# A 160-column last slot, chosen on chip, in an attention, mixture-of-experts and maxout kernel

## The chip, the cores and the metric

The kernel runs on one core of one Trainium2 chip. The metric is the device time of one execution in microseconds (us). The five engines run their own instruction streams in order: TensorE (PE, with its weight loads as PEld), VectorE (DVE), ScalarE (ACT), GpSimd (POOL) and SyncE (SP, which here issues DMAs).

## The reference

Three stages follow one another on 3072 tokens (4 sequences of 768) of width 384, all in float32:

```python
state = w * state + k_t v_t          # recurrent linear attention, 8 heads of 48
y_t = r_t @ (state + u * k_t v_t)
logits = x @ w_gate + modality_bias[modality_id]
e_idx = argmax(logits)               # one of 8 experts for each token
out[mask] = gate_w[mask] * (relu(x[mask] @ w1[e]) @ w2[e])      # 384 -> 1024 -> 384
h = maximum(maximum(x @ w1, x @ w2), x @ w3)                    # 384 -> 768
return h @ w_out                                               # 768 -> 384
```

The last stage's weights are 64-bit floats and arrive as their bit patterns; the gate's weights are scaled by 4.021, which makes the routing uneven. Worked out from the reference's own inputs (seed 0), the experts get 1569 (expert 6), 1354 (expert 5) and 149 tokens (expert 4), and the other five get none.

## The kernel before

The attention stage runs in 24 tiles of 128 tokens. After two thirds of them the most frequent expert so far is found, so that its weights are loaded while the rest of the attention runs. The expert stage then works in *slots*: a slot is one group of tokens of one expert. The first three slots (numbers 0 to 2 here) have 256 columns and belong to that expert when it has at least 768 tokens. The width of the slots behind them is chosen on chip among 256, 272, ... 384 (`WIDTHS`, nine of them) from the counts. `counting` (L607 to L645) makes that choice on DVE during slot 0: it counts how many slots each width would need, weighs them, and writes `sel`, a number that is read by all five engines (`chosen`, L1284) at the end of slot 0. The program holds one straight copy of the remaining slots for each width and each of two kinds (L1318): an *exact* copy, which has just the least number of slots that this width can need (`sure_slots`), and one which goes on in a chain of conditions. `sel` = 2 x width + kind is the number of the copy. With the counts above, 272 columns and nine slots behind the first three are chosen, the exact copy: slots 3 to 5 for the rest of expert 6, 6 to 10 for expert 5, slot 11 for expert 4.

A slot (`slot`, L1001) has eight steps. Step f makes 9 matmuls of the first layer for 128 of the 1024 hidden units (`first`, L943: three parts of 128 of the input, each as high x high, low x high and high x low of a split into two halves), which ACT (L946) and DVE (L947) turn into the high and the low half of `hid`; then 9 matmuls of the second layer for step f-1 (`second`, L955). So `hid` of step f is used one step later. Ahead of the last step the next slot's tokens are transposed on PE, three blocks of 128 at 272 columns (`turn`, L892), and split by ACT (L894) and DVE (L895). Where the slot behind belongs to another expert, each step's `renew` converts a part of that expert's weights: ACT makes the high half (L864), POOL or DVE the low half (L868).

Other work rides in the slots, handed out by position in the code: `slot` takes a list `side` and spreads it over its steps (`cum`). The list has the *conversion* of the last stage's weights (`converters`, L1029 to L1071): 24 pieces of 128 x 384, each of six jobs with seven DVE instructions (L1057 to L1068) on the landing buffers `m2raw`, and one POOL addition (L1062); and the *landing* jobs (`landing`), which work out where each result row belongs. Before, the 144 conversion jobs are spread over the nine slots 3 to 11, 16 in each; in the last slot the 24 `inv_out` matmuls (L555) stand too. The last stage (`run`) then works in six groups of 512 tokens until the end.

Each engine takes its instructions in the order of the code, so a DVE job that stands ahead of a `hid` instruction delays it.

Of the kernel before, what the change touches and what calls it, by code (L numbers as in the profile page):

```python
# [16 lines left out]
ALU = mybir.AluOpType  # L17
AX = mybir.AxisListType
# [5 lines left out]
P = 128  # L24
# [4 lines left out]
E = 8  # L29
SLOT = 256  # L30
WIDTHS = tuple(range(SLOT, SLOT + P + 1, P // 8))
NW = len(WIDTHS)
WIDE = WIDTHS[-1]
NJW = (NT - SLOT) // SLOT + 1
OWN = WIDE // P
AHEAD = 3


def last_slot(w):
    return AHEAD + (NT - SLOT - E) // w + E  # L40


def sure_slots(w):
    return AHEAD - (-(NT - AHEAD * SLOT) // w)
# [340 lines left out]
class Routing:  # L385
# [222 lines left out]
    def counting(self, wk):  # L608
        nc, V = self.nc, self.nc.vector
        tile = lambda shape, nm, dt=F32: wk.tile(shape, dt, tag=f"rt_{nm}", name=f"rt_{nm}")  # L610
        some = tile([P, 1, E], "all", BF16)
        self.tally(NTILE, some)
        cps = self.bank("cps")
        yield
        cnt = self.counts(wk, NTILE, some, cps)
        row = cnt.rearrange("p e o -> p o e")
        rem = tile([P, 1, E], "rem")
        V.tensor_tensor(rem, row, self.off, op=ALU.subtract)
        key = tile([P, 1, E], "key")
        V.scalar_tensor_tensor(key, row, float(E), self.prio, op0=ALU.mult, op1=ALU.add)  # L620
        over = tile([P, NW, E, NJW], "over", F16)
        for i in range(NW):
            V.tensor_tensor(over[:, i], rem[:, 0, :].unsqueeze(2).to_broadcast([P, E, NJW]),
                            self.wj[:, i:i + 1, :].to_broadcast([P, E, NJW]), op=ALU.is_gt)
            if i in (2, NW - 1):
                yield
        per = tile([P, NW, E], "per")
        V.tensor_reduce(per, over, axis=AX.X, op=ALU.add)
        num = tile([P, NW], "num")
        V.tensor_reduce(num, per, axis=AX.X, op=ALU.add)  # L630
        cost = tile([P, NW], "cost")
        V.tensor_tensor(cost, num, self.wcost, op=ALU.mult)
        yield
        V.tensor_tensor(cost, cost, self.wsel, op=ALU.add)
        least = tile([P, 1], "least")
        V.tensor_reduce(least, cost, axis=AX.X, op=ALU.min)
        pick = tile([P, NW], "pick")
        V.tensor_scalar(pick, cost, least, None, op0=ALU.is_equal)
        V.tensor_tensor(num, num, self.wsure, op=ALU.is_gt)
        V.scalar_tensor_tensor(num, self.wsel, 2.0, num, op0=ALU.mult, op1=ALU.add)  # L640
        V.tensor_tensor(num, num, pick, op=ALU.mult)
        V.tensor_reduce(least, num, axis=AX.X, op=ALU.add)
        V.tensor_copy(self.sel, least[0:1])
        self.plan = row, key, per, pick
        yield  # L645
# [169 lines left out]
class Experts:  # L815
# [5 lines left out]
    def open(self, st):  # L821
        tc = self.tc
        pool = st.enter_context(tc.tile_pool(name="mx", bufs=1))
        self.xg = [[pool.tile([P, DM], F32, name=f"xg{i}_{a}") for a in range(2)] for i in range(2)]
        self.xh, self.xl = ([pool.tile([P, KC, WIDE], F32R, name=f"{q}0")] for q in ("xh", "xl"))
        self.raw = (pool.tile([P, KC, FF], F32, name="raw1"), pool.tile([P, KF, DM], F32, name="raw2"))
        self.w = {nm: pool.tile(shape, F32R, name=f"w_{nm}")
                  for nm, shape in (("h1", [P, KC, FF]), ("l1", [P, KC, FF]), ("h2", [P, KF, DM]), ("l2", [P, KF, DM]))}
        self.hid = pool.tile([P, 4 * WIDE], F32R, name="hid")

# [47 lines left out]

    def gather(self, k, n=WIDE):
        for a in range(-(-n // P)):  # L880
# [32 lines left out]
    def open_more(self, pool):  # L913
        for i in range(2):
            self.xg[i] += [pool.tile([P, DM], F32, name=f"xg{i}_{a}") for a in range(2, OWN)]
        self.xh.append(pool.tile([P, KC, WIDE], F32R, name="xh1"))
        self.xl.append(pool.tile([P, KC, WIDE], F32R, name="xl1"))

# [79 lines left out]
        if job is not None:  # L998
            job(f)

    def slot(self, k, n, stop, total, side=()):  # L1001
        r = self.regs(k, stop)
        sure = sure_slots(n)

        def when(i, what):
            if i < min(sure, stop):
                what()
            elif i < stop:
                with self.tc.If(total > i):
                    what()  # L1010

        cum = [len(side) * c // 18 for c in (0, 3, 6, 9, 12, 15, 17, 18, 18)]
        for f in range(KF):
            if f == KF - 1:
                when(k + 1, lambda: self.turn(k + 1, n))
            self.step(k, f, n, r)
            if f == 0:
                when(k + 2, lambda: self.gather(k + 2, n))
            for j in side[cum[f]:cum[f + 1]]:
                j()  # L1020
        self.tail = (k, n, r)
# [178 lines left out]
def build(tc, aps):  # L1200
    nc = tc.nc
    ET = mybir.EngineType
    with ExitStack() as st:
# [4 lines left out]
        with tc.manual_schedule(), ExitStack() as right, ExitStack() as left:  # L1208
            att = Attention(tc, aps, const, ps, dram, x_dram)
            moe = Experts(tc, aps, att.ident, ps, x_dram)  # L1210
# [4 lines left out]
            route = moe.rt = Routing(tc, const, ps)  # L1215
            mo = MaxOut(tc, aps, route, ps)
            side = route.setup()
            every = (ET.PE, ET.Activation, ET.DVE, ET.Pool, ET.SP)
# [8 lines left out]
            for s in range(NTILE):  # L1227
                att.step(s, hook)
                if s == EARLY + 1:
                    for _ in side:  # L1230
                        pass
                    side = route.opening(rw, att.logits, att.bias, EARLY, lambda: moe.load_all(
                        moe.value(route.toptab[:, 0:1], (ET.SP,), E - 1)))
# [19 lines left out]
            def during(f):  # L1253
                if f < 3:
                    moe.split(f + 1, 0, nc.gpsimd)
                    moe.split(f + 1, 1)
                if f == 0:
                    with tc.If(odd > 0):
                        att.restore(EARLY, NTILE)
                    tally.append(route.choose(rw, att.logits, att.bias, EARLY, NTILE))  # L1260
                    next(tally[0])
                if f == 1:
                    next(tally.pop(), None)
                    top.close()
                    m2 = right.enter_context(tc.tile_pool(name="m2", bufs=1, side="right", reuse_waits="tile"))
                    moe.open_rows(m2)
                    moe.open_more(left.enter_context(tc.tile_pool(name="mx2", bufs=1, reuse_waits="tile")))
                    tally.append(brief.enter_context(tc.tile_pool(name="rq", bufs=1, reuse_waits="tile")))
                    tally.append(route.counting(tally[0]))
                if f > 1:  # L1270
                    next(tally[1], None)
                if f == 3:
                    moe.fetch_early(2)
                if f == 5:
                    with tc.If(moe.many > 0):
                        moe.turn(1)
# [4 lines left out]
            for _ in tally:  # L1281
                pass
            moe.tail = (0, SLOT, still)
            chosen = moe.value(route.sel, every, 2 * NW - 1)  # L1284
            ahead = lambda: tc.switch_hint({e: chosen for e in every}, 2 * NW, "width")
            with tc.If(moe.many > 0) as both:
                places = route.placing(rw)
                for k in range(1, AHEAD):
# [18 lines left out]
            total = moe.tab(0, NSLOT, every, NSLOT)  # L1307
# [7 lines left out]
            conv = mo.converters(left.enter_context(tc.tile_pool(name="m2tmp", bufs=1, reuse_waits="tile")))  # L1315
            jobs, finals = route.landing(mo.land, att.logits)

            for i in tc.Switch({e: chosen for e in every}, 2 * NW, "width"):  # L1318
                n, exact = WIDTHS[i // 2], i % 2 == 0
                sure = sure_slots(n)  # L1320
                stop = sure if exact else last_slot(n)
                moe.tail = (AHEAD - 1, SLOT, moe.regs(AHEAD - 1, stop))
                for k in range(AHEAD, sure):
                    a, b = (len(conv) * q // (sure - AHEAD) for q in (k - AHEAD, k - AHEAD + 1))
                    c, d = (len(jobs) * q // (sure - AHEAD - 1) for q in (k - AHEAD, k - AHEAD + 1))
                    side = conv[a:b]
                    for q, j in enumerate(jobs[c:d]):
                        side.insert(7 * q + 3, j)
                    if k == sure - 1:
                        for q, j in enumerate(finals):  # L1330
                            side.insert(3 * q + 1, j)
                    moe.slot(k, n, stop, total, side)
                if exact:
                    moe.end()
                    continue

                def more(k):
                    if k == stop:
                        moe.end()
                        return  # L1340
                    tail = moe.tail
                    with tc.If(total > k) as going:
                        moe.slot(k, n, stop, total)
                        more(k + 1)
                    moe.tail = tail
                    with going.Else():
                        moe.end()

                more(sure)
# [55 lines left out]
```

## Time and profile before

| | |
|---|---|
| median of 3 runs (lowest to highest) | 710.0 us (706.09 to 712.63) |
| the profiled execution | 708.11 us |
| its span, first to last instruction | 706.4 us |
| mean granted TensorE clock | 0.986 |
| PE, DVE, POOL, ACT busy | 95%, 58%, 34%, 33% of the span |
| expert slots 0 to 11 | from 146.1 to 396.0 us of the span |
| last stage | from 401 us to the end |

The PE share is of overlapping, pipelined matmuls: what a matmul costs is read from the distance between starts (in the chain of waits, nine matmuls in a row of 1.13 us are 125 ns each), not from its own duration.

### The profile page before, as it was taken

How to read it: one execution, taken by the hardware profiler on the slowest of the kernel's cores; microseconds unless marked ns; L12 is line 12 of the kernel's file. 1: busy time of each engine (PE TensorE's matmuls, PEld its weight loads, DVE VectorE, ACT ScalarE, POOL GpSimd, SP SyncE). 2: the span in 40 equal slices, each digit the busy share in tenths (PEclk: the TensorE clock that was granted, in tenths of full speed). 3: DMA queues.
4: the chain of work that ended last, by engine and by line, in shares of the span. 5: the costliest groups of instructions: out<-in, count | busy, mean ns of one | idle time of the engine just before them, and what ended most of it. 6: DMA issues, size and time to landing. Idle time of an engine off the chain costs nothing.

```text
span 706.4 us, 13754 instructions
## 1 busy us (share of the span) xinstructions
PE 669.1 (95%) x5046; PEld 598.5 (85%) x5046; DVE 409.7 (58%) x849; ACT 230.2 (33%) x545; POOL 238.8 (34%) x257
## 2 busy tenths in 40 slices
PE   8898998998989999999999899999999999999995
PEld 4787876788988989999989788888888888888884
DVE  6999998867647788777696655222222222322321
ACT  3765763652222243222242343221121221211211
POOL 6877764372033258323165211120210210210202
PEclk9999998999999999999999999999999999999998
DMA  8988867510024551333721000000100100100101
GB/s 219 299 251 249 267 196 225 193 52 23 1 73 124 169 168 55 110 97 88 217 68 47 3 1 0 12 34 0 46 0 1 45 0 1 45 0 1 45 0 46
DMA packets 36253, 61.33 MB, mean 87 GB/s; under 512 B 4881, under 2 KB 24977, under 8 KB 36161
## 3 DMA queue, kind: packets, MB, share of 16 engines
q1 hardware_dynamic: 32512, 49.02, 23.2%
q0 software_dynamic: 3648, 11.21, 5.1%
q8 instruction: 43, 0.70, 0.4%
q14 instruction: 50, 0.40, 0.2%
HBM read 50.77 MB, written 9.44 MB: 85 GB/s over the span
## 4 chain that ended last, share of the span: by engine, by line
PE 44%; issue 11%; DVE 2%; POOL 1%; ACT 0%; POOLq 0%; DVEq 0%; ACTq 0%
PE l L1135 24%; PE o L1160 7%; PE acc L955 6%; PE h L943 6%; POOL out_dram L1171 1%; PE inv_out L555 1%; PE t L892 0%; DVE m2wo L1065 0%; DVE hid L947 0%; DVE m2wl L1099 0%; DVE x2l L1099 0%; POOL x2l L1122 0%; PE acc L892 0%; POOLq L1401 0%; DVE m2wo L1057 0%
## 5 line engine op out<-in xcount | busy, mean ns | idle before, releaser
L1139 DVE TENSOR_TENSOR tm<-tm,l 128x512 f32<-128x512 f32 x72 | 49.4, 687 | 174.5 <-PE l L1135 174.5
L955 PE MATMUL acc<-hid,w_h 128*128 128x272 f32 (+1 forms) x576 | 124.9, 290 | 7.4 <-DVE hid L947 5.8
L1135 PE MATMUL l<-x2h,m2wh 128*128 128x512 f32 x324 | 126.2, 390 | 1.8 <-ACT m2wh L1103 1.8
L1135 PE MATMUL l<-x2l,m2wh 128*128 128x512 f32 x324 | 127.5, 395 | 0.4 <-DVE x2l L1099 0.4
L1135 PE MATMUL l<-x2h,m2wl 128*128 128x512 f32 x324 | 126.9, 393 | 0.5 <-DVE m2wl L1099 0.5
L955 PEld LDWEIGHTS acc<-hid,w_h 128*128 128x128 f32 x576 | 96.1, 189 | 10.6 <-DVE hid L947 8.6
L943 PE MATMUL h<-xh,w_h 128*128 128x272 f32 (+1 forms) x288 | 84.8, 295 | 2.7 <-ACTq L1308 1.9
L946 ACT ACTIVATE hid<-h 128x272 fp32r<-128x272 f32 (+1 forms) x96 | 37.9, 394 | 148.4 <-PE h L943 130.6
L943 PE MATMUL h<-xl,w_h 128*128 128x272 f32 (+1 forms) x288 | 82.7, 287 | 0.5 <-DVE xl L895 0.5
L943 PE MATMUL h<-xh,w_l 128*128 128x272 f32 (+1 forms) x288 | 82.8, 287 | 0.3 <-POOL w_l L868 0.3
L955 PE MATMUL acc<-hid,w_l 128*128 128x272 f32 (+1 forms) x288 | 82.5, 287 | 0.0
L1171 POOL DMA_INDIRECT out_dram<-o,row x24 | 23.6, 985 | 160.0 <-ACT o L1168 154.5
L1135 PEld LDWEIGHTS l<-x2h,m2wh 128*128 128x128 f32 x324 | 61.1, 189 | 13.9 <-ACT m2wh L1103 2.0
L1135 PEld LDWEIGHTS l<-x2h,m2wl 128*128 128x128 f32 x324 | 60.9, 188 | 13.7 <-DVE m2wl L1099 1.0
L1135 PEld LDWEIGHTS l<-x2l,m2wh 128*128 128x128 f32 x324 | 61.3, 189 | 13.0 <-DVE x2l L1099 0.9
L1142 ACT CAST hh<-tm 128x512 fp32r<-128x512 f32 x36 | 22.4, 622 | 149.6 <-DVE tm L1139 149.6
L947 DVE SCALAR_TENSOR_TENSOR hid<-h,hid 128x272 fp32r<-128x272 f32 (+1 forms) x96 | 41.5, 432 | 44.9 <-ACT hid L946 40.5
L224 ACT ACTIVATE A<-ident,dot 128x128 f32<-128x128 f32 x192 | 58.7, 390 | 9.0 <-DVE dot L218 8.8
L943 PEld LDWEIGHTS h<-xh,w_h 128*128 128x128 f32 x288 | 54.6, 190 | 3.4 <-issue 3.1
L943 PEld LDWEIGHTS h<-xl,w_h 128*128 128x128 f32 x288 | 54.5, 189 | 0.9 <-DVE xl L895 0.9
L943 PEld LDWEIGHTS h<-xh,w_l 128*128 128x128 f32 x288 | 54.4, 189 | 0.7 <-POOL w_l L868 0.5
L875 POOL DMA_INDIRECT xg<-x_rows,gidx x33 | 31.7, 961 | 68.7 <-PE h L943 39.7
(274 smaller groups left out, 1226.7 us busy)
## 6 DMA issues: line engine op xcount, KB each, us to landing
raw<-in_moe_w_dram SPq DMA_DIRECT2D x24, 384.0 KB, 4.3
m2raw<-in_moe_w_dram SPq DMA_DIRECT2D x18, 384.0 KB, 3.1
kT<-in_kT_dram SPq DMA_DIRECT2D x24, 224.0 KB, 4.1
rT<-in_rT_dram SPq DMA_DIRECT2D x24, 224.0 KB, 4.6
kn<-in_kn_dram SPq DMA_DIRECT2D x24, 192.0 KB, 4.4
rn<-in_rn_dram SPq DMA_DIRECT2D x24, 192.0 KB, 4.7
vn<-in_vn_dram SPq DMA_DIRECT2D x24, 192.0 KB, 4.5
x_rows<-x SPq DMA_DIRECT2D x24, 192.0 KB, 3.0
```

Source lines behind the costliest of these rows:

```text
L224: nc.scalar.mul(t["A"][:, h % 2, h // 2, :], self.ident, t["dot"][:, h:h + 1])
L555: self.nc.tensor.matmul(inv, lhsT=self.lo[:, i, :], rhs=hi[:, :, i], start=(i == 0), stop=(i == n - 1), skip_group_check=True)
L875: self.nc.gpsimd.indirect_dma_start(out=self.xg[k % 2][a], out_offset=None, in_=self.x_dram[0:rows, :], in_offset=bass.IndirectOffsetOnAxi ...
L943: nc.tensor.matmul(ps, lhsT=s[w][:, c, fs], rhs=x[:, c, :], start=(i == 0), stop=(i == 3 * KC - 1))
L946: nc.scalar.activation(hh, ps, AF.Relu)
L947: nc.vector.scalar_tensor_tensor(hl, ps, 0.0, hh.bitcast(F32), op0=ALU.max, op1=ALU.subtract)
L955: nc.tensor.matmul(self.bank[c][:, 0:n], lhsT=s[w][:, f, v], rhs=x, start=(f == 0 and q == 0), stop=(f == KF - 1 and q == 2), skip_group_c ...
L1135: nc.tensor.matmul(ps, lhsT=w[:, m, c, fs], rhs=x[:, c, :], start=(n == 0), stop=(n == 3 * KC - 1))
L1139: nc.vector.tensor_tensor(t, t, ps, op=ALU.max)
L1142: nc.scalar.copy(hh, t)
L1160: self.nc.tensor.matmul(self.acc[a], lhsT=x[:, v], rhs=w[:, f, :], start=(f == 0 and q == 0), stop=(f == NF - 1 and q == 2))
L1171: nc.gpsimd.indirect_dma_start(out=self.out[n], out_offset=bass.IndirectOffsetOnAxis(ap=self.rt.row[:, n:n + 1].bitcast(U32), axis=0), in_ ...
```

## The change

A third kind of copy is added for each width. It is exact, but its last slot has `NARROW` = 160 columns. `counting` works out, for each width, whether the last expert's last slot holds more than 160 tokens (`fill`, sixteen more DVE instructions, and one more pause among its steps, for which the whole of it starts one step earlier in slot 0: `if f > 0`). `sel` becomes 3 x width + kind, and the 27 copies are numbered by it. In the new copies the last slot gets 160 columns, its tokens are transposed in two blocks instead of three, and the conversion jobs are spread over the eight slots 3 to 10 (`wide`), 18 in each; the last slot gets none. In the other copies the spread stays.

```diff
+NARROW = SLOT // 2 + 32
...
-        V.scalar_tensor_tensor(num, self.wsel, 2.0, num, op0=ALU.mult, op1=ALU.add)
+        lk, lm = tile([P, 1, E], "lk"), tile([P, 1], "lm")
+        V.tensor_scalar(lk, rem, 0.0, 1e9, op0=ALU.is_le, op1=ALU.mult)
+        V.tensor_tensor(lk, lk, key, op=ALU.add)
+        V.tensor_reduce(lm, lk, axis=AX.XY, op=ALU.min)
+        V.tensor_scalar(lk, lk, lm, None, op0=ALU.is_equal)
+        yield
+        pl = tile([P, NW, E], "pl")
+        V.tensor_tensor(pl, per, lk.to_broadcast([P, NW, E]), op=ALU.mult)
+        fill = tile([P, NW], "fill")
+        V.tensor_reduce(fill, pl, axis=AX.X, op=ALU.add)
+        V.tensor_scalar(fill, fill, -1.0, None, op0=ALU.add)
+        V.tensor_tensor(fill, fill, self.wv, op=ALU.mult)
+        V.tensor_tensor(lk, lk, rem, op=ALU.mult)
+        V.tensor_reduce(lm, lk, axis=AX.XY, op=ALU.add)
+        V.tensor_scalar(lm, lm, float(NARROW), None, op0=ALU.subtract)
+        V.tensor_scalar(fill, fill, lm, None, op0=ALU.is_lt)
+        V.scalar_tensor_tensor(num, num, 2.0, fill, op0=ALU.mult, op1=ALU.max)
+        V.scalar_tensor_tensor(num, self.wsel, 3.0, num, op0=ALU.mult, op1=ALU.add)
...
-    def slot(self, k, n, stop, total, side=()):
+    def slot(self, k, n, stop, total, side=(), after=None, sure=0):
...
-                when(k + 1, lambda: self.turn(k + 1, n))
+                when(k + 1, lambda: self.turn(k + 1, after))
...
-                if f > 1:
+                if f > 0:
                     next(tally[1], None)
...
-            for i in tc.Switch({e: chosen for e in every}, 2 * NW, "width"):
-                n, exact = WIDTHS[i // 2], i % 2 == 0
+            for i in tc.Switch({e: chosen for e in every}, 3 * NW, "width"):
+                n, exact, last = WIDTHS[i // 3], i % 3 < 2, NARROW if i % 3 == 0 else WIDTHS[i // 3]
                 sure = sure_slots(n)
+                wide = sure - AHEAD - (last == NARROW)
...
-                    a, b = (len(conv) * q // (sure - AHEAD) for q in (k - AHEAD, k - AHEAD + 1))
+                    a, b = (len(conv) * min(q, wide) // wide for q in (k - AHEAD, k - AHEAD + 1))
...
-                    moe.slot(k, n, stop, total, side)
+                    moe.slot(k, n if k < sure - 1 else last, stop, total, side, last if k == sure - 2 else n, sure)
```

Three places show what it moves. The first is DVE in slot 0, between the `hid` of step 6 and that of step 7, before:

```order
L634 TENSOR_TENSOR rt_cost<-rt_cost,wsel 128x9
L636 TENSOR_REDUCE rt_least<-rt_cost 128x1
L638 TENSOR_SCALAR rt_pick<-rt_cost,rt_least 128x9
L639 TENSOR_TENSOR rt_num<-rt_num,wsure 128x9
L640 SCALAR_TENSOR_TENSOR rt_num<-wsel,rt_num 128x9
L641 TENSOR_TENSOR rt_num<-rt_num,rt_pick 128x9
L642 TENSOR_REDUCE rt_least<-rt_num 128x1
L643 CAST sel<-rt_least 1x1
```

The same engine, from the `hid` of step 6 on, in the changed kernel:

```order
L965 SCALAR_TENSOR_TENSOR hid<-h_6_3610,hid 128x256
L648 TENSOR_TENSOR rt_pl<-rt_per,rt_lk 128x72
L650 TENSOR_REDUCE rt_fill<-rt_pl 128x9
L651 TENSOR_SCALAR rt_fill<-rt_fill 128x9
...
L657 SCALAR_TENSOR_TENSOR rt_num<-rt_num,rt_fill 128x9
L658 SCALAR_TENSOR_TENSOR rt_num<-wsel,rt_num 128x9
L659 TENSOR_TENSOR rt_num<-rt_num,rt_pick 128x9
L660 TENSOR_REDUCE rt_least<-rt_num 128x1
L661 CAST sel<-rt_least 1x1
L965 SCALAR_TENSOR_TENSOR hid<-h_7_3646,hid 128x256
```

The first four of the eight rows above, and the four new ones on `lk`, now stand one step earlier, ahead of the `hid` of step 6; thirteen stand where eight did.

The second place is DVE in slot 10 from its `hid` of step 3 to that of step 6, in the copy that is taken (`land` is a landing job, `w_l` the next expert's weights), before:

```order
L947 SCALAR_TENSOR_TENSOR hid<-h_3_15506,hid 128x272
L1057 TENSOR_SCALAR m2wo<-m2raw_4491 128x384
L551 TENSOR_TENSOR land<-land 128x576
L1065 SCALAR_TENSOR_TENSOR m2wo<-m2raw_4491,m2wo 128x384
L947 SCALAR_TENSOR_TENSOR hid<-h_4_15536,hid 128x272
L1066 SCALAR_TENSOR_TENSOR m2wo<-m2raw_4491,m2wo 128x384
L1067 TENSOR_SCALAR m2raw_4491<-m2raw_4491 128x384
L1068 TENSOR_SCALAR m2raw_4491<-m2raw_4491 128x384
L947 SCALAR_TENSOR_TENSOR hid<-h_5_15565,hid 128x272
```

And in the changed kernel, up to the `hid` of step 5:

```order
L965 SCALAR_TENSOR_TENSOR hid<-h_3_18353,hid 128x272
L552 TENSOR_TENSOR land<-land 128x576
L1085 TENSOR_SCALAR m2raw_4508<-m2raw_4508 128x384
L1086 TENSOR_SCALAR m2raw_4508<-m2raw_4508 128x384
L965 SCALAR_TENSOR_TENSOR hid<-h_4_18382,hid 128x272
L1078 SCALAR_TENSOR_TENSOR m2wo<-m2raw_4508,m2wo 128x384
L1079 TENSOR_SCALAR m2raw_4508<-m2raw_4508 128x384
L1075 TENSOR_SCALAR m2wo<-m2raw_4509 128x384
L1083 SCALAR_TENSOR_TENSOR m2wo<-m2raw_4509,m2wo 128x384
L965 SCALAR_TENSOR_TENSOR hid<-h_5_18413,hid 128x272
```

A slot holds 21 conversion instructions instead of 18 or 19 (168 in all, over eight slots instead of nine), so single steps get one more.

The third place is PE where slot 11 starts: the last matmuls that slot 10 makes in its step 7 and what follows, before and, behind it, in the changed kernel:

```order
L955 MATMUL acc_3384<-hid,w_l_86 128x272
L955 MATMUL acc_3384<-hid,w_h_85 128x272
L943 MATMUL h_0_15664<-xh_3459,w_h_83 128x272
L943 MATMUL h_0_15664<-xl_3460,w_h_83 128x272
L943 MATMUL h_0_15664<-xh_3459,w_l_84 128x272
```

```order
L973 MATMUL acc_3384<-hid,w_l_86 128x272
L973 MATMUL acc_3384<-hid,w_h_85 128x272
L961 MATMUL h_0_18507<-xh_3459,w_h_83 128x160
L961 MATMUL h_0_18507<-xl_3460,w_h_83 128x160
L961 MATMUL h_0_18507<-xh_3459,w_l_84 128x160
```

All 144 matmuls of slot 11 now have 160 columns; their number and their weight loads stay.

## Rows read from the trace of the kernel before

**Rows 1.** The page, engines: busy us, share of the span, instructions.

```profile
PE 669.1 (95%) x5046; PEld 598.5 (85%) x5046; DVE 409.7 (58%) x849; ACT 230.2 (33%) x545; POOL 238.8 (34%) x257
```

**Rows 2.** Stretches of slots 0, 3, 4, 5, 6, 9, 10, 11: busy us of each engine.

```profile
core 0: us, PE busy (x) PEld busy (x) DVE busy (x) ACT busy (x) POOL busy (x), PEclk, DMA share, GB/s
146.10:166.60 20.50, 18.20 (x145) 17.13 (x143) 16.66 (x43) 9.15 (x18) 14.61 (x20) 1.00 0.12 40
...
205.00:228.50 23.50, 20.26 (x157) 19.35 (x157) 14.96 (x38) 5.41 (x15) 6.06 (x7) 1.00 0.38 112
228.50:247.90 19.40, 19.36 (x156) 19.14 (x154) 15.46 (x40) 5.22 (x15) 5.80 (x6) 1.00 0.54 166
247.90:270.20 22.30, 19.78 (x156) 19.12 (x154) 19.36 (x33) 9.28 (x19) 13.20 (x14) 1.00 0.46 143
270.20:291.20 21.00, 19.96 (x156) 19.30 (x155) 17.71 (x35) 7.17 (x18) 14.24 (x16) 1.00 0.30 86
...
329.30:348.40 19.10, 19.10 (x155) 19.04 (x155) 13.02 (x31) 5.17 (x14) 5.77 (x6) 1.00 0.65 181
348.40:372.50 24.10, 22.38 (x174) 21.50 (x172) 21.50 (x39) 11.67 (x24) 13.06 (x15) 1.00 0.34 104
372.50:396.00 23.50, 23.39 (x176) 21.93 (x176) 13.83 (x34) 5.10 (x13) 8.38 (x10) 1.00 0.09 28
```

**Rows 3.** Chain of waits in order of time: start us, us, what.

```profile
290.36 0.66 PE t L892 x6
...
292.46 1.13 PE acc L955 x9
...
371.95 0.55 DVE xl L895
...
400.59 12.44 PE l L1135 x48
...
415.14 6.16 PE l L1135 x27
```

**Rows 4.** PE in order of time in slot 2, nine 256-column matmuls apart.

```profile
184.95 0.28 PE L943 MATMUL h<-xh,w_h 128*128 128x256 f32 x1
...
186.03 0.28 PE L955 MATMUL acc<-hid,w_h 128*128 128x256 f32 x1
```

**Rows 5.** Conversion instructions (tile `m2raw`) in slots 5, 6, 9, 10: busy us.

```profile
247.90:270.20 22.30, 12.19 (x18) 2.05 (x2) 1.00 0.46 143
270.20:291.20 21.00, 10.26 (x20) 3.08 (x3) 1.00 0.30 86
...
329.30:348.40 19.10, 7.71 (x18) 2.92 (x3) 1.00 0.65 181
348.40:372.50 24.10, 12.08 (x19) 3.18 (x3) 1.00 0.34 104
```

**Rows 6.** PE groups in slot 5 and in slot 10: busy, mean ns, idle before.

```profile
L955 PE MATMUL acc<-hid,w_h 128*128 128x272 f32 x48 | 10.7, 294 | 2.5 <-DVE hid L947 2.5
...
L955 PE MATMUL acc<-hid,w_h 128*128 128x272 f32 x54 | 12.1, 294 | 1.5 <-DVE hid L947 1.4
...
L943 PE MATMUL h<-xl,w_h 128*128 128x272 f32 x28 | 8.2, 291 | 0.3 <-DVE xl L895 0.3
```

**Rows 7.** The end of slot 0 in order of time, DVE and then PE.

```profile
164.57 0.16 DVE L634 TENSOR_TENSOR rt_cost<-rt_cost,wsel 128x9 f32<-128x9 f32 x1
...
165.98 0.40 DVE L947 SCALAR_TENSOR_TENSOR hid<-h,hid 128x256 fp32r<-128x256 f32 x1
...
166.62 0.38 PE L943 MATMUL h<-xh,w_h 128*128 128x256 f32 x1 [0.82 <-DVE hid L947]
```

**Rows 8.** The page, DMA issues of expert weights: count, KB each, us.

```profile
raw<-in_moe_w_dram SPq DMA_DIRECT2D x24, 384.0 KB, 4.3
```

**Rows 9.** Stretches of the attention and of the last stage's start.

```profile
20.00:113.00 93.00, 83.16 (x1256) 73.10 (x1255) 88.44 (x155) 60.34 (x179) 70.22 (x80) 1.00 0.85 253
...
399.90:403.30 3.40, 3.01 (x8) 2.16 (x7) 3.40 (x7) 1.22 (x3) 0.09 (x1) 0.50 0.00 0
```

More of the change, by code (lines that the diff above doesn't have):

```diff
@@ L999, in step @@
             job(f)
-    def slot(self, k, n, stop, total, side=()):
+    def slot(self, k, n, stop, total, side=(), after=None, sure=0):
         r = self.regs(k, stop)
-        sure = sure_slots(n)
+        after = after or n
         def when(i, what):
@@ L1283, in build @@
             moe.tail = (0, SLOT, still)
-            chosen = moe.value(route.sel, every, 2 * NW - 1)
-            ahead = lambda: tc.switch_hint({e: chosen for e in every}, 2 * NW, "width")
+            chosen = moe.value(route.sel, every, 3 * NW - 1)
+            ahead = lambda: tc.switch_hint({e: chosen for e in every}, 3 * NW, "width")
             with tc.If(moe.many > 0) as both:
```

## The prediction

> **What bounds the kernel now.** I read the page's engine line first: PE is busy 95% of the span, DVE 58% [rows 1]. That is an average over stages, so the next view is the table of stretches by slot [rows 2]. The reader is to see two kinds of slots in it. In slots 4 and 9 the PE column is as long as the slot (19.36 of 19.40, 19.10 of 19.10 us) and DVE has 3.9 to 6.1 us left over: PE sets the time. In slots 5 and 10, where the next expert's weights are also converted, PE has 19.78 of 22.30 and 22.38 of 24.10 us, and DVE is nearly full (19.36 and 21.50). Slots 7 and 8, not shown, look like 4 and 9. The PE groups say who is late: the second layer waits 2.5 us in slot 5 and 1.5 us in slot 10, nearly all for the low half of `hid` from DVE [rows 6]. Slot 11, which the change makes narrower, is PE's own: 23.39 of 23.50 us, DVE 13.83 [rows 2]. So the change takes work from a slot in which DVE has 9.7 us to spare, and puts it into eight slots, two of which at least have nothing to spare.
>
> **Is the narrow copy taken?** The reference's routing leaves 149 tokens for the last expert's only slot, under 160, with nine slots of 272 columns. The trace fits: 24 loads of expert weights are three experts of eight parts [rows 8]. So I take it that it is.
>
> **Slot 11, the gain.** It has 8 steps x 18 = 144 matmuls. At 272 columns nine take 1.13 us, 125.5 ns each [rows 3]. No row shows 160 columns. The nearest are 256 columns, 1.08 us for nine or 120 ns [rows 4], and 128 columns with a full 128x128 float32 weight tile, the transposes, six in 0.66 us or 110 ns [rows 3]. From 512 columns (27 in 6.16 us, 228 ns [rows 3]) to 272 a column is worth 0.43 ns; from 256 to 128 it is worth 0.08 ns. Something that doesn't shrink with the columns takes over at about 110 ns, and every matmul here brings a new weight tile. Between those two rows 160 columns come to 112.5 ns, so the gain is 144 x 13 ns = **1.9 us**; the bounds are 0.8 us (120 ns) and 2.2 us (110 ns). Three transposes fewer ahead of it give 3 x 0.11 = **0.3 us**. DVE's third `xl` block (0.55 us [rows 3]) goes too; PE waits 0.3 us for it at the end of slot 10 [rows 6], which I count: **0.3 us** (0 to 0.55). The 24 `inv_out` matmuls stay.
>
> The Trainium skill, "TensorE: Matmul & The Clock Gate", section "Back-to-back issue gap", gives a sustained 81 ns at 128 columns and 131 ns at 512. The trace doesn't agree (110 and 228 ns, float32 weights). By the page 160 columns would be some 85 ns (an estimate between its figures), slot 11 would give 5.8 us, and the sum below would be a gain of about 1.2 us.
>
> **Slot 0, a cost.** `counting` gets 16 more DVE instructions. Eight neighbours of the same size take 1.41 us from start to start, 0.18 us each [rows 7], so 16 take 2.8 us. DVE is the late one here: PE's first matmul of slot 1 comes only after the last `hid`, behind a wait of 0.82 us [rows 7]. Against this, the whole of `counting` starts one step earlier, and a step is 18 x 120 ns = 2.2 us, in which DVE had idle time (16.66 of 20.50 us busy [rows 2]). So the cost lies between 2.8 - 2.2 = 0.6 us and 2.8 us if nothing of the early start helps; I take **1.0 us**, near the lower end, since 3.8 us of idle is more than the 2.8, and keep zero as its floor. PE's small `cps` matmul moves a step with it and waits for one short reduction more, which the step ahead covers.
>
> **Conversion, a cost.** 168 DVE instructions over nine slots are 18.7 in each, over eight they are 21: 2.3 more. POOL's 24 additions and the 24 DMAs on SP move too, three to a slot instead of 2.7; POOL has 13 of 24 us busy in the fullest slot [rows 2], and its instruction makes nobody wait before the last stage, so I cost it at nothing. A conversion instruction takes 0.43 us in slot 9 (7.71 over 18) but 0.66 us in slots 5 and 10 (12.19 over 18, 12.08 over 19 [rows 5]), where POOL is busy with the next expert's weights at the same time.
> - Slots 5 and 10: DVE is full and PE waits for it, so 2.3 x 0.66 = 1.5 us each stands open. **3.0 us** together; at the quiet price 2.0, at three instructions each 4.0.
> - Slots 3 and 6: PE is short of the slot by 3.2 and 1.0 us, DVE by 8.5 and 3.3 [rows 2], most of it where no job is handed out yet. 2.3 x 0.51 us (10.26 over 20 [rows 5]) is 1.2 each; I take half: **1.2 us** together (0 to 2.4).
> - Slots 4, 7, 8 and 9: 2.3 x 0.43 = 1.0 us of work against 3.9 us or more of idle DVE and a PE that never stops: nothing. If that cover were gone it would cost 1.0 us in each.
>
> **What is late next.** In slot 11 it is still PE: DVE keeps eight `hid`, one `yt` copy and four small instructions. The last stage starts as before, behind the last `yt` copies. The switch now has 27 copies instead of 18; it is one jump by a register in either, so I cost it at nothing.
>
> **Sum:** -1.9 - 0.3 - 0.3 + 1.0 + 3.0 + 1.2 = +2.7 us against the profiled execution's 708.1 us, or 710.8 us. The median of the runs shown, 710.0, lies 1.9 above that execution; from it the sum gives 712.7. Between the two I put **711.5 us**: no change that can be measured. (I take 1%, 7 us, as what a measurement of this kernel can tell from none; its three runs alone lie 6.5 us apart.)
>
> **The rivals.**
> 1. *Columns are all that counts.* If a 160-column matmul followed the 0.43 ns per column of the wide ones, it would take 78 ns and slot 11 give 6.8 us instead of 1.9. For it: 512, 272 and 256 columns are in fair order. Against it: the 128-column row at 110 ns. The time: 711.5 - 4.9 = 706.6 us, still within 1%. Chance 0.16. The page named above would have it end near here.
> 2. *DVE has no room anywhere that matters, and the kernel gets slower.* A job delays the `hid` behind it even in a slot with idle time, if that time stands at the slot's start, where no job is queued. If slots 3 to 6 and 10 all pay 1.5 us, and slot 0 its 2.8, the sum is 7.5 + 2.8 - 2.5 = +7.8 us: 716 from the profiled execution, 718 from the median. It decides once the idle left behind the first step is below some 1.5 us in each of these. For it: DVE full in 5 and 10, 17.71 of 21 us in 6. Against it: slot 4 has 3.9 us left and PE next to no wait. Chance 0.10.
> 3. *The narrow copy isn't taken*, for a count other than I worked out. Then the spread stays at 16 jobs and only slot 0's 1.0 us is left: about 710 us. Chance 0.04.
> 4. *The clock falls in slot 11*, since PE has fewer columns to work on in the same number of instructions. At the start of the last stage, where PE waits for its first operands, a stretch of 3.4 us was granted 0.50, the lower level (1.2 GHz) [rows 9], and 48 matmuls take 12.44 us where 48 x 228 ns = 10.9 would do [rows 3]: 1.5 us for 3.4. If all of slot 11, 18 us without `inv_out`, ran so, it would cost up to 8 us: 719 us. Against it: the attention, whose matmuls have at most 128 columns, holds the upper level (1.00, 2.4 GHz) over 93 us [rows 9]. Chance 0.05. The Trainium skill, same page, section "Why this matters for your kernels", warns that thin matmuls let the clock swing, which speaks against a narrower slot; the attention's rows here don't agree.
>
> The forecast keeps 0.65.
>
> **Range and chances.** All terms at their good ends give -2.2 - 0.3 - 0.55 + 0 + 2.0 + 0 = -1.1 us, at their bad ends -0.8 - 0.3 + 2.8 + 4.0 + 2.4 = +8.1. With the spread of the runs the range is 705 to 717; it takes in rival 1, rival 3 and the near half of rival 2. Faster by over 1% would need rival 1 and no cost at all besides: 0.04. Slower by over 1%: most of rivals 2 and 4 less what noise hides, 0.10. Within 1%: 0.86.
>
> **What would show it.** In the trace after: nine matmuls of 160 columns in 1.0 us (rival 1: 0.70); slot 11 shorter by about 2 us; slots 5 and 10 longer by 1 to 2 us each, with 21 conversion instructions and a longer wait for `hid`; slots 4, 7, 8, 9 still at 19.1 to 19.4; the first matmul of slot 1 about 1 us later; the granted clock 1.00 in slot 11. The prediction is wrong if slot 11 gives over 4 us, if the quiet slots grow, or if slots 5 and 10 take the extra work without a longer wait.

## The result, and the profile after

On the chip of the prediction the changed kernel takes 714.06 us (median of 21 executions) against 710.0 us before: a ratio of 1.0053, interval 1.0032 to 1.0074, or +3.8 us. That is slower, by less than the 1% named as what can be told from no change, and inside the range; but the interval lies clear of no change, so it is a change that can be measured. Two more sessions on other chips gave 1.0108 (1.0062 to 1.0154) and 1.0084 (1.0054 to 1.0115), there +6 to +8 us, the first of them over the 1%. 6 of the 34 timed executions of the changed kernel lie 12 to 17 us above the rest, the one whose trace was taken with the result among them; the ratios leave them out, and the profile shown here is that of another execution of the same kernel, on another chip ("All of it" below).

The page's engine line, as in [rows 1]:

```profile
PE 671.7 (94%) x5043; PEld 600.4 (84%) x5043; DVE 413.6 (58%) x861; ACT 228.6 (32%) x544; POOL 240.8 (34%) x257
```

Twelve more instructions on DVE: thirteen for the choice, one fewer for the third `xl` block. The diff adds fourteen and takes one away, 21 rows where 8 were; the sixteen of the text ahead and of the prediction is a miscount. The stretches of slots 0, 3, 4, 5, 6, 9, 10 and 11, as in [rows 2] (the slots start elsewhere in this execution, and each stretch here begins with the slot's first matmul):

```profile
144.80:166.60 21.80, 17.98 (x146) 17.14 (x144) 19.38 (x56) 9.18 (x18) 14.60 (x20) 1.00 0.12 37
213.50:235.60 22.10, 21.51 (x153) 20.82 (x154) 15.17 (x36) 5.42 (x14) 5.97 (x6) 0.92 0.36 101
235.60:255.90 20.30, 19.57 (x156) 19.19 (x155) 16.99 (x42) 5.20 (x13) 6.41 (x6) 1.00 0.66 203
255.90:280.10 24.20, 20.54 (x155) 19.28 (x154) 20.06 (x33) 10.14 (x20) 15.02 (x17) 1.00 0.34 109
280.10:302.70 22.60, 20.18 (x156) 19.31 (x155) 19.57 (x39) 6.17 (x15) 13.30 (x14) 1.00 0.28 80
341.50:360.50 19.00, 19.00 (x155) 19.00 (x154) 15.22 (x34) 5.21 (x13) 6.01 (x6) 1.00 0.74 219
360.50:381.70 21.20, 19.62 (x153) 18.95 (x151) 18.24 (x32) 10.18 (x19) 12.66 (x14) 1.00 0.25 77
381.70:406.40 24.70, 22.67 (x179) 21.52 (x177) 6.32 (x19) 4.55 (x13) 6.23 (x9) 0.93 0.01 2
```

In [rows 2] the stretches of slots 3 to 10 begin a step early, at the last step of the slot ahead. So slot 10's 24.1 us hold 18 matmuls of slot 9, and slot 3's 23.5 us hold the wait ahead of that slot. From its first matmul slot 3 took 21.3 us before, and slot 10 this:

```profile
350.62:371.97 21.35, 19.85 (x155) 19.19 (x154) 19.05 (x34) 10.29 (x20) 12.54 (x14) 1.00 0.27 83
```

The lengths of the other slots there are right to 0.3 us. DVE is emptied in the last slot (13.83 to 6.32 us) and filled in the others; slot 6 is 1.6 us longer, slot 9 not at all. The narrow slot, from which 2.5 us were to come, isn't shorter than before: 24.7 us. The chain of waits in slot 11 says why. First the wait, then the matmuls:

```profile
382.08 0.88 DVE m2raw L1079
382.96 0.94 DVE xl L913 x2
383.94 1.57 PE h L961 x8
385.51 2.12 PE acc L973 x9
387.63 0.68 PE inv_out L556 x4
388.31 0.97 PE h L961 x9
389.28 1.00 PE acc L973 x9
```

From 388 us on nine matmuls of 160 columns take 0.97 to 1.00 us where nine of 272 took 1.13 [rows 3]: the gain is there. But the slot starts late, behind DVE's `xl`, and its first two groups take 1.57 and 2.12 us: a stretch at the lower clock level. PE in order of time at that place, with the wait in brackets, and the stretch:

```profile
383.94 0.34 PE L961 MATMUL h<-xl,w_h 128*128 128x160 f32 x1 [2.03 <-DVE xl L913]
```

```profile
384.40:387.90 3.50, 3.50 (x18) 3.31 (x18) 0.77 (x2) 0.93 (x3) 1.72 (x3) 0.51 0.00 0
387.90:406.40 18.50, 18.50 (x158) 17.72 (x156) 3.01 (x12) 3.40 (x10) 2.11 (x3) 1.00 0.01 2
```

That wait of 2.03 us was 0.3 us before [rows 6].

### The profile page after: what moved, and what is told of

Its sections match the earlier page's. It is cut to its first block, busy times and chain, and to the rows that moved or that the text cites. A ratio compares the mean times of both kernels' runs of the same rounds, so it can differ in the third digit from the quotient of the medians.

```text
span 724.2 us, 13775 instructions
## 1 busy us (share of the span) xinstructions
PE 683.6 (94%) x5037; PEld 615.6 (85%) x5043; DVE 413.4 (57%) x861; ACT 229.6 (32%) x544; POOL 239.6 (33%) x257
## 4 chain that ended last, share of the span: by engine, by line
PE 45%; issue 10%; DVE 2%; POOL 1%; ACT 0%; POOLq 0%; DVEq 0%; ACTq 0%
PE l L1153 23%; PE o L1178 7%; PE acc L973 7%; PE h L961 6%; POOL out_dram L1189 1%; PE inv_out L556 1%; PE t L910 0%; DVE hid L965 0%; DVE m2raw L1085 0%; DVE m2wo L1084 0%; POOL x2l L1140 0%; PE acc L910 0%; POOLq L1420 0%; DVE w_l L886 0%; DVE m2raw L1079 0%
## 5 line engine op out<-in xcount | busy, mean ns | idle before, releaser
L973 PE MATMUL acc<-hid,w_h 128*128 128x272 f32 (+2 forms) x576 | 133.3, 304 | 7.0 <-DVE hid L965 6.4
L973 PEld LDWEIGHTS acc<-hid,w_h 128*128 128x128 f32 x576 | 104.3, 206 | 9.7 <-DVE hid L965 8.7
L961 PE MATMUL h<-xh,w_h 128*128 128x272 f32 (+2 forms) x288 | 88.3, 307 | 2.3 <-ACTq L1326 1.9
L961 PE MATMUL h<-xl,w_h 128*128 128x272 f32 (+2 forms) x288 | 86.5, 300 | 3.9 <-DVE xl L913 3.9
L964 ACT ACTIVATE hid<-h 128x272 fp32r<-128x272 f32 (+2 forms) x96 | 37.1, 386 | 160.9 <-PE h L961 144.2
L973 PE MATMUL acc<-hid,w_l 128*128 128x272 f32 (+2 forms) x288 | 86.9, 302 | 0.0
L961 PE MATMUL h<-xh,w_l 128*128 128x272 f32 (+2 forms) x288 | 86.4, 300 | 0.3 <-POOL w_l L886 0.3
L965 DVE SCALAR_TENSOR_TENSOR hid<-h,hid 128x272 fp32r<-128x272 f32 (+2 forms) x96 | 40.5, 422 | 61.2 <-ACT hid L964 59.0
L961 PEld LDWEIGHTS h<-xl,w_h 128*128 128x128 f32 x288 | 58.7, 204 | 4.3 <-DVE xl L913 4.3
L973 PEld LDWEIGHTS acc<-hid,w_l 128*128 128x128 f32 x288 | 59.1, 205 | 0.0
```

The lines of the kernel that those rows point to most:

```text
L961: nc.tensor.matmul(ps, lhsT=s[w][:, c, fs], rhs=x[:, c, :], start=(i == 0), stop=(i == 3 * KC - 1))
L964: nc.scalar.activation(hh, ps, AF.Relu)
L965: nc.vector.scalar_tensor_tensor(hl, ps, 0.0, hh.bitcast(F32), op0=ALU.max, op1=ALU.subtract)
L973: nc.tensor.matmul(self.bank[c][:, 0:n], lhsT=s[w][:, f, v], rhs=x, start=(f == 0 and q == 0), stop=(f == KF - 1 and q == 2), skip_group_c ...
```

## The experiments

### The change in its parts

Three kernels of which each leaves out a part, and the changed kernel, on one chip. They tell what the choice, the narrow slot and the spread cost or give by themselves. The choice alone:

```diff
-                n, exact, last = WIDTHS[i // 3], i % 3 < 2, NARROW if i % 3 == 0 else WIDTHS[i // 3]
+                n, exact, last = WIDTHS[i // 3], i % 3 < 2, WIDTHS[i // 3]
-                wide = sure - AHEAD - (last == NARROW)
+                wide = sure - AHEAD
```

> The longer choice in slot 0 and the 27 copies alone: last slot of 272 columns, 16 jobs in each of nine slots. Theory A: +1.0 us against before (1.0014), in slot 0. If the third kind of copies or the switch cost something, it is more and not in slot 0. Theory C: as A, unless the wait at the end of slot 0 is long enough for a stretch at the lower level.

Choice and narrow slot, without the new spread:

```diff
-                wide = sure - AHEAD - (last == NARROW)
+                wide = sure - AHEAD
```

> The narrow last slot, but the conversion stays spread over nine slots, 16 jobs in each. Theory A: the gain of slot 11 (1.9 + 0.3 + 0.3) less slot 0's 1.0, so -1.5 us against before (0.998), and 4.2 us faster than the changed kernel. Rival B: -6 us (0.991). Theory C: PE's wait ahead of slot 11 stays as short as before (0.3 us), no long stretch at the lower level in slot 11 in any execution; otherwise as A.

Choice and spread, without the narrow slot:

```diff
-                n, exact, last = WIDTHS[i // 3], i % 3 < 2, NARROW if i % 3 == 0 else WIDTHS[i // 3]
+                n, exact, last = WIDTHS[i // 3], i % 3 < 2, WIDTHS[i // 3]
-                wide = sure - AHEAD - (last == NARROW)
+                wide = sure - AHEAD - (i % 3 == 0)
```

> The conversion over eight slots, 18 jobs in each, and the longer choice, but a last slot of 272 columns. Theory A: +1.0 (slot 0) + 4.2 (slots 3, 5, 6, 10) = +5.2 us against before (1.007). Rival B: the same, since it concerns the narrow slot alone. Theory C: the waits of about 2 us ahead of slot 11 are there as in the changed kernel, and so may be short stretches at the lower level, but with 272 columns the clock comes back at once.

All of it (no edit):

> The changed kernel once more, for an execution whose last slot runs at the upper clock level and for the distance to the others on one chip. Theory A (the sum of the prediction): +2.7 us against before (ratio 1.004), slot 11 about 2 us shorter with nine 160-column matmuls in 1.0 us, slots 5 and 10 1.5 us longer each, slot 0 1.0 us longer. Rival B (columns are all that counts): nine in 0.70 us and slot 11 7 us shorter. Theory C (the clock): the costs are mostly stretches at the lower level behind waits of PE; then the granted clock of this run is below before's 0.986 by more than 0.003 and the stretches lie behind waits of about 2 us.

Then the kernel before, one execution for its trace, on another chip:

> The kernel before, for a trace from the chip of these runs. Theory A: slot 0 about 1 us shorter than in the kernel with the longer choice alone, everything else within 0.3 us. If the wait ahead of slot 3 is 4.2 us here as well, instead of the 1.9 us of the first trace, it belongs to the chip and not to the 27 copies; if it is 1.9 us, the copies cost 2.3 us that the prediction put at nothing.

Ratios to before: the choice alone 1.0041 (1.0011 to 1.0071), choice and narrow slot 0.9987 (0.9958 to 1.0016), choice and spread 1.0127 (1.0083 to 1.0171), all 1.0108 (1.0062 to 1.0154). That is +2.9, -0.9, +9.1 and +7.7 us where the sum of the prediction gave +1.0, -1.5, +5.2 and +2.7: the intervals of the first two hold it, those of the two with the spread lie above it. The slots in their traces, from the first matmul of one to that of the next (slot 11 to its last matmul), in us; slots 1 and 2 are left out here:

| slot | before (again) | choice | choice, narrow | choice, spread | all |
|---|---|---|---|---|---|
| 0 | 20.53 | 21.43 | 22.71 | 22.70 | 21.77 |
| 3 | 21.89 | 21.64 | 21.37 | 22.05 | 22.10 |
| 4 | 19.91 | 20.03 | 19.98 | 20.23 | 20.27 |
| 5 | 23.12 | 23.30 | 23.10 | 24.17 | 24.26 |
| 6 | 20.94 | 20.90 | 20.92 | 22.55 | 22.55 |
| 7 | 19.44 | 19.43 | 19.41 | 19.47 | 19.41 |
| 8 | 19.23 | 19.20 | 19.04 | 19.45 | 19.39 |
| 9 | 19.04 | 19.04 | 19.04 | 19.02 | 19.03 |
| 10 | 21.36 | 21.39 | 21.05 | 21.38 | 21.15 |
| 11 | 23.78 | 23.82 | 21.51 | 25.72 | 24.75 |

The narrow slot gives 23.82 - 21.51 = 2.3 us in slot 11 and 0.3 in slot 10: the 2.5 us of the prediction. Its first two groups of matmuls, with choice and narrow slot:

```profile
381.92 1.12 PE h L961 x8
383.04 1.16 PE acc L973 x9
```

By the ratios the gain is more, 0.9987 against 1.0041 or some 4 us. The spread costs 0.4 + 0.2 + 0.9 + 1.65 + 0.25 in slots 3 to 8 and 1.9 in slot 11, 5.3 us together (by the ratios 1.0127 against 1.0041, some 6 us), where 4.2 were forecast. Slot 0, 1.3 us longer in that trace, isn't counted: the two have the same choice there, and the section on the choice says what differs. Slot 10 doesn't pay its share itself. PE's first matmul on `xl` in slot 11, of the choice alone and then of choice and spread:

```profile
385.75 0.39 PE L961 MATMUL h<-xl,w_h 128*128 128x272 f32 x1 [0.26 <-DVE xl L913]
```

```profile
388.82 0.39 PE L961 MATMUL h<-xl,w_h 128*128 128x272 f32 x1 [2.18 <-DVE xl L913]
```

DVE is late at the end of slot 10, because step 6 of that slot now holds three conversion instructions ahead of the `xl` blocks instead of one. Slot 5 does the same to slot 6, with three instead of two. PE's first matmul on `xl` in slot 6, of the same two kernels:

```profile
285.78 0.39 PE L961 MATMUL h<-xl,w_h 128*128 128x272 f32 x1 [0.24 <-DVE xl L913]
```

```profile
285.82 0.39 PE L961 MATMUL h<-xl,w_h 128*128 128x272 f32 x1 [1.05 <-DVE xl L913]
```

So 0.8 of slot 6's 1.65 us is slot 5's delay. Slot 6's own part is longer waits for `hid` (0.86 and 0.49 us where they were 0.47 and 0.26).

The conversion instructions of the same groups, slots 5, 6, 9 and 10 of the changed kernel, as in [rows 5]:

```profile
255.90:280.10 24.20, 14.74 (x21) 2.21 (x2) 1.00 0.34 109
280.10:302.70 22.60, 10.25 (x21) 4.11 (x4) 1.00 0.28 80
341.50:360.50 19.00, 10.02 (x21) 3.12 (x3) 1.00 0.74 219
360.50:381.70 21.20, 12.85 (x20) 2.98 (x2) 1.00 0.25 77
```

21 instructions at 0.70 us in slot 5 and 0.64 in slot 10: the price was right. In slot 9 they cost 2.3 us of DVE more (7.71 to 10.02) and the slot 0: the cover held there.

The kernel before has the long wait ahead of slot 3 on these chips too (1.9 us on the chip of the prediction), so these 4.2 us aren't the 27 copies:

```profile
218.10 0.56 PE L943 MATMUL h<-xh,w_h 128*128 128x272 f32 x1 [4.28 <-ACTq L1308]
```

Slot 2 ahead of it isn't quite the same, though. It was 27.9 us long in that trace and 28.5 to 28.7 in the nine of changed kernels with the choice in slot 0 on these chips (on the chip of the prediction 24.56 before and 24.68 after). PE waits longer there for ACT's half of `hid`, before and then with the choice alone (`issue`: it waited for nothing that the profile shows):

```profile
212.27 0.38 PE L955 MATMUL acc<-hid,w_h 128*128 128x256 f32 x1 [0.36 <-issue]
```

```profile
214.54 0.39 PE L973 MATMUL acc<-hid,w_h 128*128 128x256 f32 x1 [1.28 <-ACT hid L964]
```

That is 0.6 to 0.8 us which the prediction put at nothing. Whether the 27 copies are the reason stays open: there is one trace of the kernel before on these chips. With slot 0's 0.9 us it brings the choice alone nearer to its ratio, 1.0041 or +2.9 us (0.8 to 5.1).

### How a matmul's cost goes with its columns

```diff
-... NARROW if i % 3 == 0 else WIDTHS[i // 3]
+... 224 if i % 3 == 0 else WIDTHS[i // 3]
```

on the kernel with choice and narrow slot (one execution, for its trace).

> The narrow copy with 224 instead of 160 columns in its last slot, conversion over nine slots: the distance between matmuls at a third width. Theory A (something that does not shrink with the columns takes over near 110 ns): 224 columns lie close to 256 (120 ns), at 116 to 119 ns, nine in 1.05 to 1.07 us. Rival B (columns alone, 0.43 ns each): 105 ns, nine in 0.95 us.

The chain of waits in its slot 11:

```profile
384.09 1.00 PE h L961 x9
385.09 1.00 PE acc L973 x9
```

111 ns at 224 columns, the same as at 160 (0.97 to 1.00 us for nine). Both expectations miss: it isn't columns alone, nor is it a slope between 128 and 256. From 128 to 224 columns the cost is flat, at 108 to 111 ns; 256 take 120. Slot 11 was 21.64 us long with 224 columns and 21.51 with 160.

### What the choice costs in slot 0, and where else it can stand

The choice alone, begun one step later:

```diff
-                if f > 0:
+                if f > 1:
                     next(tally[1], None)
```

> The longer choice alone (last slot of 272 columns, 16 jobs in each of nine slots), but begun in step 2 of slot 0 as before, not one step earlier. Theory A: without the earlier start the sixteen instructions cost their full 2.8 us at the end of slot 0: slot 0 at 23.3 us, no wait of 1.8 us in its middle, +2.8 us against before (1.004). Rival: the earlier start only moves the wait to the middle of the slot, where it calls up a stretch at the lower level; without it slot 0 is no longer than 22.0 us and the time nearer to before (1.002).

1.0081 (1.005 to 1.0112), where 1.004 was expected. Slot 0 took 23.36 us, as expected (20.53 + 2.8 = 23.3). PE at the start of slot 1, and the stretch that followed:

```profile
175.99 0.58 PE L961 MATMUL h<-xh,w_h 128*128 128x256 f32 x1 [3.64 <-DVE sel L661]
```

```profile
174.00:180.80 6.80, 4.81 (x29) 4.73 (x30) 2.72 (x14) 1.13 (x3) 0.00 (x0) 0.50 0.01 2
```

So what PE waits for there is `sel` itself, which all engines read before slot 1. That the 2.8 us came out is partly luck: the thirteen instructions took 2.5 us (0.19 each), and PE's first matmul then came 0.58 us after `sel`, where it had come 0.24 us after the last `hid`. The stretch at the lower level makes slot 1 2.1 us longer (20.41 against 18.33), which with slot 2's 0.8 us is why the kernel lost more than 2.8 us. The earlier start is worth having, as the prediction assumed, though it also brings a wait of 1.8 us into the middle of slot 0. The choice alone there:

```profile
165.61 0.51 PE L973 MATMUL acc<-hid,w_h 128*128 128x256 f32 x2 [1.73 <-DVE hid L965]
...
173.36 0.38 PE L961 MATMUL h<-xh,w_h 128*128 128x256 f32 x1 [1.69 <-DVE hid L965]
```

The wait in the middle can cost more than this trace shows. In nine traces with the choice in slot 0 it was 1.7 to 1.8 us. In seven of them a stretch of 3.4 us at the lower level began behind it, and slot 0 took 22.1 to 22.7 us; in the other two (the choice alone, 1.73 us, and the changed kernel again, 1.83 us) there was none, and slot 0 took 21.4 and 21.8.

Then the new instructions taken out of slot 0, on the kernel with choice and narrow slot (`kinds` holds them and the three behind them, up to the write of `sel`, and `chosen` is read ahead of slot 3 instead of slot 1; shortened):

```diff
+                        if k == AHEAD - 1 and f in (1, 2):
+                            next(kinds)
...
-            chosen = moe.value(route.sel, every, 3 * NW - 1)
...
+            chosen = moe.value(route.sel, every, 3 * NW - 1)
             total = moe.tab(0, NSLOT, every, NSLOT)
```

> Narrow last slot, conversion over nine slots, and the sixteen instructions of the choice moved from slot 0 to slot 2 (steps 1 and 2, where DVE has little), with the number of the copy read at the end of slot 2 instead of slot 0. Theory A: slot 0 is again as long as before or shorter by the 0.8 us that PE waited at its end; -2.5 to -3.5 us against before (0.9955). If slot 0's cost is not the sixteen instructions but the 27 copies, it stays at 0.9987 as with the choice in slot 0.

0.9975 (0.9947 to 1.0003). Slot 0 is 19.56 us long, 1.0 us shorter than before and 1.9 to 3.2 us shorter than with the choice in it; slot 11 21.52. But slot 2, where the choice now stands, is 29.0 us long, 0.4 more than with the choice in slot 0 and 1.1 more than before. 0.9955 was expected; the interval holds it, and no change as well. This is the best version that I found, together with the last one below, but it can't be told from the version with the choice in slot 0 (0.9987).

### The spread the other way round

15 jobs in slots 3 to 10 and 24 in slot 11, first with the choice in slot 0, then with the late choice:

```diff
-                    a, b = (len(conv) * min(q, wide) // wide for q in (k - AHEAD, k - AHEAD + 1))
+                    a, b = (5 * len(conv) * q // (5 * wide + 3) if q < wide else len(conv) for q in (k - AHEAD, k - AHEAD + 1))
```

> Narrow last slot, longer choice in slot 0, and the spread turned round: 15 conversion jobs in each of slots 3 to 10, 24 in slot 11. Theory A: the cost of the spread runs both ways: 1.2 instructions fewer in slots 5 and 10 (0.8 us each) and in 3 and 6 (0.3 each) give 2 us against the same kernel with 16 jobs in each (0.9987), so 0.996; slot 11 has DVE work of some 17 us in 21 and stays PE's. If the spread's cost comes only past a threshold at 18 jobs, nothing is gained (0.9987).

> Narrow last slot, the choice in slot 2, and 15 conversion jobs in slots 3 to 10 with 24 in slot 11: the two edits that the runs so far point to, together. Theory A: slot 0 at 19.6 us as with the late choice, slots 4 and 5 each 1 us shorter than with 16 jobs, slot 11 1 us longer: 1 us less than the late choice alone, 0.9965 of before. Rival: the longer waits in slot 11 take all of it back, 0.9975 or more.

1.0002 (0.9976 to 1.0029) and 0.9974 (0.9946 to 1.0001). The first misses its expectation (0.996), the second lands on the rival's (0.9975), with an interval that holds both. Slot 5 is 1.1 us and slot 4 0.7 us shorter than with 16 jobs (21.95 and 19.25 against 23.10 and 19.98 us), but slot 11 is 0.9 us longer (22.39), and with the late choice slots 6 and 10 lose 0.7 together: nothing is left that can be measured.

### The lower clock level in the narrow slot

The changed kernel with 224 columns in its last slot, and once more as it is, on one chip:

```diff
-... NARROW if i % 3 == 0 else WIDTHS[i // 3]
+... 224 if i % 3 == 0 else WIDTHS[i // 3]
-                wide = sure - AHEAD - (last == NARROW)
+                wide = sure - AHEAD - (i % 3 == 0)
```

> The changed kernel with 224 instead of 160 columns in its last slot. Theory A: slot 11 0.2 us longer than with 160 columns (144 x 1.5 ns), otherwise the changed kernel. Theory C: PE's wait of 2 us ahead of slot 11 is there as well, but with 224 columns the clock comes back after one stretch; no execution stays at the lower level through slot 11 as the first trace of the changed kernel did.

> The changed kernel beside these three on one chip. Theory A: 1.005 to 1.011 of before, about the time of the one with 224 columns. Theory C: some of its executions lie 12 to 15 us above the others, with slot 11 at the lower level (144 matmuls of 213 ns instead of 111), which the one with 224 columns doesn't have.

1.0076 (1.0045 to 1.0107) and 1.0084 (1.0054 to 1.0115). The stretches of slot 11 with 224 columns:

```profile
382.40:385.70 3.30, 1.30 (x12) 1.10 (x11) 2.52 (x5) 0.24 (x1) 3.00 (x5) 1.00 0.00 0
385.70:389.10 3.40, 3.40 (x18) 3.17 (x18) 0.83 (x2) 1.96 (x4) 1.11 (x2) 0.50 0.00 0
389.10:407.20 18.10, 18.10 (x153) 17.17 (x151) 3.55 (x12) 2.85 (x8) 2.11 (x3) 1.00 0.01 1
```

And with 160, in its traced execution on that chip:

```profile
387.40:391.40 4.00, 1.98 (x17) 1.80 (x17) 2.80 (x6) 0.51 (x2) 3.71 (x6) 1.00 0.00 0
391.40:424.70 33.30, 33.30 (x164) 32.43 (x162) 3.70 (x14) 4.03 (x11) 2.49 (x4) 0.50 0.00 1
```

Both have the wait of 2.0 us for `xl` ahead. Choice and spread with 272 columns has it too (2.18 us, above), and its slot 11 ran at the upper level throughout. With 224 columns the upper level was back after 3.4 us; with 160 it didn't come back in this execution before the last stage, though PE never stood still. Two of the seven executions with 160 columns were 15 us above the others, none of the seven with 224. Seven are few, and the execution shown with the result did come back (0.51 for 3.5 us, then 1.00, above): that fewer columns are the reason is likely, and not shown. The wait has better evidence: with 160 columns and without the new spread, so without the wait of 2 us, none of 48 executions of four kernels lay that far above the others, against 6 of 34 of the changed kernel (two of these six were traced, and slot 11 is where both lost the time).

## Why the prediction was right

**The size and the sign.** +2.7 us were summed; +3.8 (2.3 to 5.3) were measured on the same chip, and +6 to +8 on two others. The mechanism is the one forecast: DVE work moved from a slot where it cost nothing into slots where it did, for a gain of 2.5 us. But the range of 12 us was wide, "no change that can be measured" was wrong, and on the two other chips the sum missed by 3 to 5 us, nearer to rival 2's +7.8 (though not by its 1.5 us in each of five slots). Of the signs named in the prediction some failed: in the changed kernel slot 11 wasn't shorter and its granted clock was 0.93, not 1.00; and one of the quiet slots, slot 4, grew by 0.2 to 0.4 us.

**Slot 11's gain** was 2.3 + 0.3 us against 1.9 + 0.3 + 0.3. It was right to take the 128-column row as the nearest and not the slope of the wide ones; rival 1 is excluded by the rows, nine matmuls in 0.97 to 1.00 us and not 0.70, and a slot 11 shorter by 2.3 us and not 6.8. Rival 3 is out too: the matmuls of slot 11 do have 160 columns. The straight line between 128 and 256 columns was wrong, though: the cost is flat to 224. In the whole change the gain was lost again: slot 11 was 1.0 us longer than before.

**The Trainium skill's figure** for sustained matmuls (85 ns at 160 columns, as estimated in the prediction from the page "TensorE: Matmul & The Clock Gate", section "Back-to-back issue gap") is not what this kernel shows: 108 to 111 ns.

**Slot 0's cost** was 0.9 us in the choice alone and 1.2 in the changed kernel, against 1.0, where no stretch at the lower level fell into it, and 2.2 us in the two traces of the table where one did. One did in seven of nine traces (1.6 to 2.2 us), so 1.0 us was too little for most executions. The run without the earlier start bears out that this start takes back a good part of the 2.8 us (23.36 us against 21.4 to 22.7); the 2.8 us itself rests on the miscount of sixteen and on leaving out PE's reading of `sel`, two errors that cancelled.

**The conversion** is the term that was mis-sized: 4.2 us against 5.3 in the traces. Slots 5 and 10 were put at 3.0 us. In slot 5 they cost 0.9, at the start of slot 6 another 0.8, and at the start of slot 11 1.9: 3.6 together, and not where I looked for it. Slot 10 itself took the extra work without a longer wait for `hid`; its delay went into the next slot's `xl`. Slots 3 and 6 were put at 1.2 us and cost 0.4 and, without slot 5's delay, 0.85; slot 3's 3.2 us of idle PE, read from a stretch that began too early, were 1.3. Slots 4, 7, 8 and 9, put at nothing, cost 0.45: a little of rival 2's mechanism.

**Rival 4** got 0.05 with the argument that the attention holds the upper level with 128 columns. That argument looked at the columns alone. The lower level came behind waits of 1.7 to 2.1 us, of which the change makes two new ones, in slot 0 and ahead of slot 11. A stretch of 3.4 us behind the second cost 1.4 us (the first two groups took 1.57 + 2.12 us, with choice and narrow slot alone 1.12 + 1.16), and with the wait of 2 us it took back more than the narrow slot gave. In the two executions traced among the six that lie high, nearly all of slot 11 ran at the lower level and took 37.3 and 37.4 us, nearly 13 more than the 24.75 of the table. The rival's price for that, up to 8 us, was too low, because it took 18 us as the length of the slot at the lower level too.

## What to carry to other kernels

A narrower matmul pays only down to the width below which its cost stays flat; look in the trace for the narrowest full matmul of the same kind, and cut no deeper than the columns that it shows to count (here 224 would have done). Before work is moved out of a slot that is to become shorter, ask which engine ends the slots that receive it, and look at what stands behind the last job of each: here it was an operand of the next slot (`xl` of slots 6 and 11) that came late. A decision computed on chip costs at the place where the engines read it. Reading it later freed slot 0 here and cost part of that again where it was moved to.

## What the runs showed of the hardware

- With a new 128x128 float32 weight tile for each, matmuls of 128 (the transposes), 160 and 224 columns all take 108 to 111 ns, of 256 columns 120, of 272 125.
- The lower clock level came behind waits of PE of 1.7 to 1.8 us in the middle of slot 0 in seven of nine traces, and behind waits of 2.0 to 2.2 us ahead of slot 11 in four of five; no trace without such a wait fell in the middle of slot 0 or in slot 11. How long the wait was doesn't decide it: 1.72 us (224 columns, choice and narrow slot) was followed by a stretch, 1.83 us (the changed kernel again) and 2.18 us (choice and spread) were not.
- At the lower level nine 160-column matmuls take 1.88 to 1.92 us, nearly twice as much as at the upper one (0.97 to 1.00), in the first trace of the changed kernel:

```profile
386.42 1.89 PE h L961 x9
388.31 1.92 PE acc L973 x9
```

Why the upper level came back after one stretch in one traced execution with 160 columns, and only after 41 us in the two others, stays open.
